# The opening of a two-layer kernel: whole first weight slab on ScalarE's queue, x tile 0 alone, and SyncE held by a dummy matmul

## The chip, the cores and the metric

One core of a Trainium2 chip runs the kernel. Its engines are TensorE (PE in the profile, its weight loads PEld), ScalarE (ACT), VectorE (DVE), GpSimd (POOL) and SyncE (SP); here SyncE only issues transfers. The metric is device time in microseconds (us), the median of several runs. Before the change it is 124.7 us (three runs, 124.55 to 125.05).

## The reference

```python
B, S, D, F = 1, 2048, 640, 1728          # all bfloat16
h = jnp.einsum("bsd,df->bsf", x, w1)     # x: (1, 2048, 640), w1: (640, 1728)
h = silu(h)
out = jnp.einsum("bsf,fd->bsd", h, w2)   # w2: (1728, 640)
```

## The kernel before

The contraction of the first product, D = 640, is cut into five k-tiles of 128. `xT` holds x turned, k on the partitions, and is filled by transposing transfers, which SyncE issues. `w1s` holds w1 with k on the partitions; a "slab" is the first 1024 columns of one k-tile (eight column tiles of 128, 256 KB). The 2048 rows are worked in four chunks of 512; an "x tile" below is one k-tile of the first chunk (512 rows by 128, 128 KB).

**The opening (first chunk).** Weights and x arrive in pieces, so the first chunk is worked k by k: for k = 0 to 4, TensorE goes over the eight column tiles and adds each product into that column's PSUM bank (`part`, `sweep`, `opening`). Each column tile is a pair of matmuls, one for each half of 64 columns (`step`). Step k waits for slab k and x tile k. After step 4 each bank goes through ScalarE's Silu into `hT`. Then come the remaining columns (`ld_rest`, `ld_rest2`), where one bank runs over all five k at once, then chunks 1 to 3 the same way, the last 64 columns, and the second product with its stores.

**Dummies.** Until the data is there TensorE multiplies a zeroed tile `z` (`first_dummies`): 13 full matmuls of 128 x 256 and one pair of half width.

**The order of the early work.** `early` takes what was just emitted and puts it ahead of the start barrier of its engine, so it runs at once. Each engine runs its own list in order. SyncE's list of early transfers is: x tiles 0 and 1 in one transposing transfer (L123); the last three eighths of slab 0 (L148); slabs 1 and 2 (L149, L150); x tile 2; slab 3; x tiles 3 and 4 in one; slab 4; then the rest of w1 in two pieces (L156, L157). After the barrier follow the transposing transfers of the other chunks (L163) and w2. ScalarE's early list is the first five eighths of slab 0 (L124) and a Silu on a small tile, which loads the activation table. All transfers of plain kind go through the helper `load` and so carry line 88; the early transposes carry line 93; all products carry line 175, the dummies line 132. A `wait` makes the engine's next instruction wait for a semaphore's value; each transfer has its own semaphore.

Of the kernel before, what the change touches and what calls it, by code (L numbers as in the profile page):

```python
# [9 lines left out]
def bass_standalone__dense_activation_silu__prompt_kernel(  # L10
# [13 lines left out]
    P = 128  # L24
    NB = 8
    BANK = 512
    DT = D // P
    FT = F // P
    FL = F - FT * P
    SCH = 512  # L30
    HB = 256
# [7 lines left out]
    pe, act, dve, pool, sp = nc.tensor, nc.scalar, nc.vector, nc.gpsimd, nc.sync  # L39

    with ExitStack() as es:
        def sb(name, shape, dtype):
            return es.enter_context(nc.sbuf_tensor(name, shape, dtype))
# [10 lines left out]
        z = sb("z", [P, HB], bf16)  # L54
        ps = es.enter_context(nc.psum_tensor("ps", [P, NB, BANK], fp32))
# [4 lines left out]
        def sem(name):  # L60
            s = es.enter_context(nc.semaphore(name))
            count[s.name if hasattr(s, "name") else name] = 0
            return [s, 0]

        def tick(ins, s, n=1):
            ins.then_inc(s[0], n)
            s[1] += n
            return (s, s[1])

        def wait(eng, *points):  # L70
            for pt in points:
                if pt is None:
                    continue
                s, v = pt
                key = (id(eng), id(s))
                if seen.get(key, 0) < v:
                    eng.wait_ge(s[0], v)
                    seen[key] = v

        s_pe, s_act, s_dve = sem("s_pe"), sem("s_act"), sem("s_dve")  # L80
# [4 lines left out]
        def load(eng, out_ap, in_ap):  # L85
            s = sem(f"s_ld{n_dma[0]}")
            n_dma[0] += 1
            return tick(eng.dma_start(out=out_ap, in_=in_ap), s, 16)

        def turned(c0, c1, k0, k1):  # L90
            s = sem(f"s_tr{n_dma[0]}")
            n_dma[0] += 1
            return tick(sp.dma_start_transpose(
                out=xT[:, k0:k1, c0:c1], in_=xf[c0:c1, k0 * P:k1 * P]), s, 16)

        ET = mybir.EngineType

        def early(emit, engine, arrived=True):
            n = len(nc.main_func.blocks[0].instructions)
            r = emit()  # L100
            lst = nc.main_func.blocks[0].instructions
            new = lst[n:]
            del lst[n:]
            at = next(
                i for i, ins in enumerate(lst)
                if ins.opcode == ("EventSemaphore" if arrived else "Drain") and ins.engine == engine
            )
            lst[at:at] = new
            return r
# [2 lines left out]
        w2_v = w2[0:F0, :].rearrange("(ft p) d -> p ft d", p=P)  # L112

        NO = NB
        NA = 5
        CO = NO * P

        def slab(eng, k, f0=0, f1=NO):
            return load(eng, w1s[:, k, f0 * P:f1 * P], w1_v[:, k, f0 * P:f1 * P])

        ld_w1 = {}
        ld_t = {}
        ld_t[0] = ld_t[1] = early(lambda: turned(0, SCH, 0, 2), ET.SP, False)  # L123
        ld_w1[0] = early(lambda: slab(act, 0, 0, NA), ET.Activation, False)  # L124
        p_z = early(lambda: tick(dve.memset(z[:, :], 0.0), s_dve), ET.DVE, False)  # L125

        bank_free = [None] * NB
# [1 line left out]
        def dummies(n, w):  # L129
            for _ in range(n):  # L130
                for c0 in range(0, P, w):
                    pe.matmul(ps[c0:c0 + w, 3, 0:HB], lhsT=z[:, 0:w], rhs=z[:, :],  # L132
                              start=True, stop=True)

        def first_dummies():
            wait(pe, p_z)
            dummies(13, P)
            dummies(1, HC)

        p_warm = early(lambda: tick(pool.memset(warm[:, :], 0.0), s_pool), ET.Pool, False)  # L140
# [4 lines left out]

        early(warm_up, ET.Activation, False)

        ld_w1b = early(lambda: slab(sp, 0, NA, NO), ET.SP, False)  # L148
        ld_w1[1] = early(lambda: slab(sp, 1), ET.SP, False)  # L149
        ld_w1[2] = early(lambda: slab(sp, 2), ET.SP, False)  # L150
        ld_t[2] = early(lambda: turned(0, SCH, 2, 3), ET.SP, False)
        ld_w1[3] = early(lambda: slab(sp, 3), ET.SP, False)
        ld_t[3] = ld_t[4] = early(lambda: turned(0, SCH, 3, DT), ET.SP, False)
        ld_w1[4] = early(lambda: slab(sp, 4), ET.SP, False)
        CM = CO + 2 * P
        ld_rest = early(lambda: load(sp, w1s[:, :, CO:CM], w1_v[:, :, CO:CM]), ET.SP, False)  # L156
# [17 lines left out]
        def mm(o, l, r, start, stop, shared=False):  # L174
            return pe.matmul(o, lhsT=l, rhs=r, start=start, stop=stop, skip_group_check=shared)  # L175
# [7 lines left out]
        def step(b, k, ft, c0, c1, start=False, stop=False):  # L183
            for h0 in (0, HC):
                ins = mm(ps[h0:h0 + HC, b, :], w1s[:, k, ft * P + h0:ft * P + h0 + HC],
                         xT[:, k, c0:c1], start, stop, shared=True)
            return ins

        def part(k, ft, c0, c1, start=False, stop=False):
            return step(ft, k, ft, c0, c1, start, stop)  # L190

        def sweep(k, c0, c1, *waits):
            wait(pe, *waits)
            for ft in range(NO):
                part(k, ft, c0, c1)

        def opening():
            first_dummies()
            wait(pe, ld_t[0], ld_w1[0])
            for ft in range(NO):  # L200
                if ft == NA:
                    wait(pe, ld_w1b)
                part(0, ft, 0, SCH, start=True)
            for k in range(1, DT - 1):
                sweep(k, 0, SCH, ld_w1[k], ld_t[k])

        early(opening, ET.PE)
        wait(pe, ld_w1[4], ld_t[4])
        for ft in range(NO):
# [12 lines left out]
        for ft in range(NO, FT):  # L222
# [3 lines left out]
            for k in range(DT):  # L226
                ins = step(b, k, ft, 0, SCH, start=(k == 0), stop=(k == DT - 1))
            silu(hT[:, ft, 0:SCH], ps[:, b, :], b, tick(ins, s_pe))
        for c in range(1, NSC):
            wait(pe, ld_xc[c])  # L230
            for ft in range(FT):
                b = bank()
                for k in range(DT):
                    ins = step(b, k, ft, c * SCH, (c + 1) * SCH, start=(k == 0), stop=(k == DT - 1))
                h_last = silu(hT[:, ft, c * SCH:(c + 1) * SCH], ps[:, b, :], b, tick(ins, s_pe))
        h_tail = []
        for q in range(NSC // 2):
            b = bank()
            for k in range(DT):
                for hh in range(2):  # L240
                    c = 2 * q + hh
                    ins = mm(ps[hh * FL:(hh + 1) * FL, b, :], w1s[:, k, F0:F],
                             xT[:, k, c * SCH:(c + 1) * SCH],
                             start=(k == 0), stop=(k == DT - 1), shared=True)
# [130 lines left out]
        for u, eng in ((A, dve), (B, act), (C, act), (E, dve), (G2, act)):  # L375
            for ft in range(FT):
                ins = u.whole(ft, ft == FT - 1)
# [30 lines left out]
```

## Time and profile before

| | |
|---|---|
| median of three runs | 124.7 us |
| profiled execution: its span, first to last instruction (the page has no other time for it) | 123.8 us |
| TensorE matmul busy | 121.3 us, 98% |
| ScalarE busy | 38.8 us, 31% |
| VectorE busy | 6.9 us, 6% |
| transfers of SyncE's queue | 10.11 MB, 34.1% of 16 DMA engines' span |
| transfers of ScalarE's queue | 0.16 MB, 0.6% |
| granted clock of TensorE, mean | 1.000 |

The profile is of one execution. A row names line, engine, operation and tile (written <- read), a count, and durations. In the view in order of time, a row gives start and duration in us, and in brackets the idle time ahead of it and what ended it; consecutive instructions of one kind are merged. An SPq or ACTq row is the issuing of a transfer, not its movement; the list of transfers gives the time from the start of the issue to the landing. In the view of stretches, a row gives the stretch, its length, an engine's busy time with its number of instructions, the granted clock, the mean share of the DMA engines and the GB/s. Some matmul records can be missing from a trace.

### The profile page before, as it was taken

The page shows a single profiled execution, that of the slowest core. Times are in us where ns is not written, and L with a number is a line of the kernel's source. Part 1 is how long each engine was busy: PE and PEld are TensorE (multiplying, and loading weights), DVE is VectorE, ACT ScalarE, POOL GpSimd, SP SyncE. Part 2 cuts the span into 40 slices and gives each one's busy share as a digit, 9 for nine tenths or more (in the row PEclk, how much of TensorE's full clock was granted, in tenths as well). Part 3 has the DMA queues.
Part 4 walks back from the last instruction along what each step waited for, and adds up shares of the span by engine and source line. Part 5 has one row for each costly group of instructions (what it writes and reads, how often), then busy time and mean ns, then how long its engine had stood idle before and what let it go on. Part 6 is the DMA issues. An engine that isn't in the chain of part 4 may idle for free.

```text
span 123.8 us, 2298 instructions
## 1 busy us (share of the span) xinstructions
PE 121.3 (98%) x1056; PEld 58.9 (48%) x1057; DVE 6.9 (6%) x11; ACT 38.8 (31%) x67; POOL 0.3 (0%) x5
## 2 busy tenths in 40 slices
PE   8999999999999999999999999999999999999993
PEld 5345545545545545545544444444444444444452
DVE  0000000000000000000000022002200300222001
ACT  4000985555555555555530011001100200110110
POOL 0000000000000000000000000000000000000000
DMA  6999974554894000000000004302200220023112
GB/s 138 239 246 331 138 86 91 100 77 107 214 394 157 0 0 0 3 5 0 0 0 5 0 0 101 74 0 105 107 0 5 106 106 0 5 106 116 53 66 82
DMA packets 19625, 10.42 MB, mean 84 GB/s; under 512 B 13728, under 2 KB 19104, under 8 KB 19616
## 3 DMA queue, kind: packets, MB, share of 16 engines
q1 hardware_dynamic: 19472, 10.11, 34.1%
q10 hardware_dynamic: 144, 0.16, 0.6%
q8 instruction: 8, 0.13, 0.5%
q14 instruction: 1, 0.01, 0.0%
HBM read 4.51 MB, written 2.62 MB: 58 GB/s over the span
## 4 chain that ended last, share of the span: by engine, by line
PE 95%; DMA 3%; ACT 0%; issue 0%
PE ps L175 95%; DMA xT<-in_x_dram 3%; ACT o_sb L256 0%
## 5 line engine op out<-in xcount | busy, mean ns | idle before, releaser
L175 PE MATMUL ps<-xT,w1s 128*64 128x512 bf16 x540 | 59.6, 384 | 0.1
L175 PE MATMUL ps<-w2s,hT 64*128 64x512 bf16 (+3 forms) x376 | 46.0, 369 | 0.2 <-issue 0.2
L175 PEld LDWEIGHTS ps<-xT,w1s 128*64 128x64 bf16 x540 | 30.0, 111 | 29.6 <-issue 1.2
L179 ACT ACTIVATE hT<-ps 128x512 bf16<-128x512 f32 x52 | 30.0, 607 | 29.9 <-PE ps L175 29.9
L175 PEld LDWEIGHTS ps<-w2s,hT 64*128 64x128 bf16 (+1 forms) x377 | 21.0, 95 | 24.2 <-issue 0.2
L256 ACT CAST o_sb<-ps 128x512 bf16<-128x512 f32 (+1 forms) x9 | 5.0, 551 | 41.5 <-PE ps L175 41.5
L175 PE MATMUL ps<-hT,w2s 64*128 64x512 bf16 x104 | 11.7, 376 | 0.0
L175 PEld LDWEIGHTS ps<-hT,w2s 64*128 64x128 bf16 x104 | 5.0, 94 | 6.3 <-issue 0.4
L254 DVE CAST o_sb<-ps 128x512 bf16<-128x512 f32 (+1 forms) x8 | 5.4, 675 | 40.5 <-PE ps L175 40.5
L254 DVE CAST oT<-ps 128x512 bf16<-128x512 f32 x2 | 1.4, 692 | 74.2 <-PE ps L175 74.2
L256 ACT CAST oT<-ps 128x512 bf16<-128x512 f32 x2 | 1.2, 586 | 10.6 <-PE ps L175 10.6
L132 PE MATMUL ps<-z 128*128 128x256 bf16 (+1 forms) x15 | 3.3, 419 | 0.4 <-DVE z L125 0.4
L175 PE MATMUL ps<-w2t,hTt 64*128 64x512 bf16 (+2 forms) x17 | 2.9, 363 | 0.0
L132 PEld LDWEIGHTS ps<-z 128*128 128x128 bf16 (+1 forms) x15 | 1.9, 142 | 1.5 <-issue 0.4
L179 ACT ACTIVATE hTt<-ps 128x512 bf16<-128x512 f32 x2 | 1.2, 598 | 1.0 <-PE ps L175 1.0
L144 ACT ACT_TABLE_LOAD x1 | 1.3, 1283 | 0.5 <-issue 0.5
L175 PEld LDWEIGHTS ps<-w2t,hTt 64*128 64x128 bf16 x17 | 0.9, 94 | 1.1
L175 PE MATMUL ps<-hTt,w2t 64*128 64x512 bf16 x4 | 0.8, 376 | 0.0
L175 PEld LDWEIGHTS ps<-hTt,w2t 64*128 64x128 bf16 x4 | 0.2, 94 | 0.2
L144 ACT ACTIVATE warm<-warm 128x32 f32<-128x32 f32 x1 | 0.2, 229 | 0.0
L125 DVE MEMSET z<- 128x128 uint32 x1 | 0.2, 165 | 0.2 <-issue 0.2
L140 POOL MEMSET warm<- 128x32 f32 x1 | 0.1, 125 | 0.0
(4 smaller groups left out, 0.4 us busy)
## 6 DMA issues: line engine op xcount, KB each, us to landing
out_dram<-o_sb SPq DMA_DIRECT2D x15, 160.0 KB, 1.8
w2s<-in_w_dram SPq DMA_DIRECT2D x1, 1120.0 KB, 6.1
w1s<-in_w_dram SPq DMA_DIRECT2D x4, 256.0 KB, 4.1
w2s<-in_w_dram SPq DMA_DIRECT2D x1, 960.0 KB, 8.2
w1s<-in_w_dram SPq DMA_DIRECT2D x1, 560.0 KB, 7.0
w1s<-in_w_dram SPq DMA_DIRECT2D x1, 320.0 KB, 5.8
xT<-in_x_dram SPq DMA_TRANSPOSE x18, 3.7
w1s<-in_w_dram ACTq DMA_DIRECT2D x1, 160.0 KB, 2.7
```

The costliest lines, as they stand in the source:

```text
L125: p_z = early(lambda: tick(dve.memset(z[:, :], 0.0), s_dve), ET.DVE, False)
L132: pe.matmul(ps[c0:c0 + w, 3, 0:HB], lhsT=z[:, 0:w], rhs=z[:, :], start=True, stop=True)
L140: p_warm = early(lambda: tick(pool.memset(warm[:, :], 0.0), s_pool), ET.Pool, False)
L144: act.activation(out=warm[:, :], in_=warm[:, :], func=ACT.Silu)
L175: return pe.matmul(o, lhsT=l, rhs=r, start=start, stop=stop, skip_group_check=shared)
L179: r = tick(act.activation(out=out_ap, in_=in_ap, func=ACT.Silu), s_act)
L254: r = tick(dve.tensor_copy(out=out_ap, in_=in_ap), s_dve)
L256: r = tick(act.copy(out=out_ap, in_=in_ap), s_act)
```

## The change

- ScalarE loads all of slab 0 in one transfer; SyncE's transfer of its last three eighths goes, and so does the wait for it after the fifth column tile.
- x tiles 0 and 1 are two transfers. Tile 0 is SyncE's first. Ahead of tile 1 SyncE waits for a semaphore that TensorE raises at the end of the fifth dummy. Then follow, in this order, tile 1, slabs 1 and 2, tile 2, slab 3, tiles 3 and 4 in one transfer, slab 4, and the rest as before. The wait stands ahead of all of these in SyncE's list.
- The full dummies are 11, five and six, where there were 13; the pair of half width stays.

```diff
-        NA = 5
         CO = NO * P
@@
-        ld_t[0] = ld_t[1] = early(lambda: turned(0, SCH, 0, 2), ET.SP, False)
-        ld_w1[0] = early(lambda: slab(act, 0, 0, NA), ET.Activation, False)
+        p_gate = (s_pe, 1)
+        ld_t[0] = early(lambda: turned(0, SCH, 0, 1), ET.SP, False)
+        ld_w1[0] = early(lambda: slab(act, 0), ET.Activation, False)
         p_z = early(lambda: tick(dve.memset(z[:, :], 0.0), s_dve), ET.DVE, False)
@@
         def dummies(n, w):
             for _ in range(n):
                 for c0 in range(0, P, w):
-                    pe.matmul(ps[c0:c0 + w, 3, 0:HB], lhsT=z[:, 0:w], rhs=z[:, :],
-                              start=True, stop=True)
+                    ins = pe.matmul(ps[c0:c0 + w, 3, 0:HB], lhsT=z[:, 0:w], rhs=z[:, :],
+                                    start=True, stop=True)
+            return ins
 
         def first_dummies():
             wait(pe, p_z)
-            dummies(13, P)
+            assert tick(dummies(5, P), s_pe) == p_gate
+            dummies(6, P)
             dummies(1, HC)
@@
-        ld_w1b = early(lambda: slab(sp, 0, NA, NO), ET.SP, False)
+        early(lambda: wait(sp, p_gate), ET.SP, False)
+        ld_t[1] = early(lambda: turned(0, SCH, 1, 2), ET.SP, False)
         ld_w1[1] = early(lambda: slab(sp, 1), ET.SP, False)
         ld_w1[2] = early(lambda: slab(sp, 2), ET.SP, False)
         ld_t[2] = early(lambda: turned(0, SCH, 2, 3), ET.SP, False)
         ld_w1[3] = early(lambda: slab(sp, 3), ET.SP, False)
-        ld_t[3] = ld_t[4] = early(lambda: turned(0, SCH, 3, DT), ET.SP, False)
+        ld_t[3] = ld_t[4] = early(lambda: turned(0, SCH, 3, 5), ET.SP, False)
         ld_w1[4] = early(lambda: slab(sp, 4), ET.SP, False)
@@
             wait(pe, ld_t[0], ld_w1[0])
             for ft in range(NO):
-                if ft == NA:
-                    wait(pe, ld_w1b)
                 part(0, ft, 0, SCH, start=True)
```

## The prediction

> **What bounds the kernel now.** I read the chain of work that ended last first, then the waits of the opening, then the opening in order of time, then stretches of it. The page's own chain and the same chain in order of time:
>
> ```profile
> PE 95%; DMA 3%; ACT 0%; issue 0%
> ```
> ```profile
> 0.00 3.78 DMA xT<-in_x_dram
> 3.78 0.04 issue
> 3.82 106.78 PE ps L175 x706
> ```
> From 3.82 us on TensorE works without a gap for 106.78 us. So the end moves only with (a) the moment of the first product, (b) TensorE's speed, (c) a gap that the change opens. What it edits lies in the first 8 us. There, in order of time (start, duration):
>
> ```profile
> 0.00 1.33 SPq L93 DMA_TRANSPOSE xT<-in_x_dram  x1
> 0.12 0.37 ACTq L88 DMA_DIRECT2D w1s<-in_w_dram  x1
> ...
> 0.39 3.31 PE L132 MATMUL ps<-z 128*128 128x256 bf16 x15 [0.39 <-DVE z L125]
> ...
> 1.39 1.54 SPq L88 DMA_DIRECT2D w1s<-in_w_dram  x3
> ...
> 2.97 1.16 SPq L93 DMA_TRANSPOSE xT<-in_x_dram  x1
> ...
> 4.17 0.58 SPq L88 DMA_DIRECT2D w1s<-in_w_dram  x1
> ...
> 4.79 1.24 SPq L93 DMA_TRANSPOSE xT<-in_x_dram  x1
> ...
> 6.07 1.62 SPq L88 DMA_DIRECT2D w1s<-in_w_dram  x3
> ```
> The two x tiles of the first transfer land at 3.78, the dummies end at 3.70, ScalarE's part of slab 0 has landed at 0.12 + 2.7 = 2.9: the x tiles are last. The next view gives TensorE's pace, by stretches (busy us, instructions):
>
> ```profile
> 5.53:5.96 0.43, 0.43 (x6) 1.00 1.98 298
> 5.96:6.30 0.34, 0.34 (x4) 1.00 0.77 115
> 6.30:6.52 0.22, 0.22 (x6) 1.00 0.81 231
> ```
> Each stretch is the pitch of one pair of products: 0.427 us up to 5.96, 0.216 from 6.30, one pair between at 0.34. The column of the granted clock says 1.00 throughout and doesn't show this. With c us at the slow pace in the mixed pair, c/0.427 + (0.34 - c)/0.216 = 1 gives c = 0.26: TensorE doubles its pace at 6.22. From 3.82 to there 5.6 of slab 0's eight pairs run slow; the step over slab 0 ends at 6.74, the later steps take 1.73 each and begin at 6.74, 8.46, 10.19 and 11.92, and the columns after the eighth begin at 13.64.
>
> **What it is measured against.** The profiled span is 123.8; the median of the runs is 124.7 (124.55 to 125.05), 0.9 more, for what lies around the span. I add the change of the span to 124.7. Half a per cent, 0.62 us, is about what a measurement of this kernel can tell from no change.
>
> **Part 1: tile 0 alone, slab 0 whole on ScalarE, two dummies fewer.** The first product waits for tile 0 and all of slab 0. The dummies took 2.89 us from 0.39 to the half pair at 3.28, 0.22 each; two fewer put that pair at 2.84, so 3.06 is the earliest start. The latest: before, 160 + 256 KB had to land for it, now 256 + 128 KB. The queues moved 241 GB/s from 1.78 to 3.30; 32 KB less is 0.14, so data at 3.64 and a start at 3.68 (the 0.04 of issue included). I take a value between. The missing tile is worth 128 KB / 241 = 0.54. ScalarE's extra 96 KB goes partly into room that stood free: in the quarters from 1.25 the rates were 128, 230 and 220 GB/s, where 286 came right after, room for (158 + 56 + 66) x 0.25 = 70 KB. Some 26 KB, 0.11, are left: 3.78 - 0.54 + 0.11 = 3.35, and I start the products there. Slab 0 with that load comes at 2.9 + 96 KB / 241 = 3.27, also before.
>
> The Trainium skill, "DMA: Bandwidth & Descriptors", Rules for kernel authors, speaks against this part: transfers issued from several engines run on the same 16 DMA engines, so spreading them saves issue time alone. By that rule, taken strictly, the start is the byte-bound 3.68. The trace doesn't decide: 416 KB arriving by 3.78 fits it, the low rate before 1.75 leaves room.
>
> Starting 0.47 earlier isn't 0.47 of the end, because those microseconds run at the slow pace. With the doubling still at 6.22: (6.22 - 3.35)/0.427 = 6.7 pairs slow, 1.3 x 0.216 = 0.28 after, the step ends at 6.50 and not 6.74: **0.24 less**. Ends: start 3.06 gives 0.38, start 3.68 gives 0.07.
>
> "TensorE: Matmul & The Clock Gate" of the Trainium skill, Part 1, says that the gate opens after a window of some 3.4 us of activity and that the windows run freely, whatever the kernel does; by it the doubling stays where it is when work is moved inside the window, so 0.24 and not 0.47. It also says the phase differs from run to run. The three runs of before lie within 0.5 us, which bears out no wide spread.
>
> **Part 2: SyncE's order.** Slab 0's last 96 KB (one issue, some 0.6 with its gap) leave the queue; tile 1 becomes an issue of its own (1.16, as the one-tile transfer at 2.97 has it), held until the fifth dummy is done: 0.39 + 4 x 0.22 + 0.42 = 1.69. SyncE would be free at 1.2 to 1.3, so 0.4 of the hold is real. Behind it everything is queued: tile 1 at 1.69 to 2.85, slab 1 at 2.91 (was 2.00), slab 2 at 3.44 (2.49), tile 2 at 3.97, slab 3 at 5.17, tiles 3 and 4 at 5.79, slab 4 at 7.07, the two rests about 7.7 and 8.2, the five transposes of the next chunk from 9.1 (8.09). So all is issued about 1.0 later. This part costs nothing as long as the landings keep ahead of TensorE; the cover is the lead that each had.
>
> From issue to landing before: slab 1 3.9, slab 2 4.1, tile 2 4.2, slab 3 4.1, tiles 3 and 4 4.4, slab 4 4.5, the rests 5.8 and 7.0. Upper end, those latencies unchanged: slab 1 lands at 6.81 against a need at 6.50, 0.31 late; tile 2 8.17 against 8.23; tiles 3 and 4 10.2 against 9.95, 0.25 late, but hidden if slab 1 was already waited for; slab 4 11.6 against 11.68; the first rest 13.5 against 13.40, the second 15.2 against 15.6. The delays don't add, the largest counts: 0.35 with the wake-up. Lower end, none: ScalarE's transfer at 0.12, with little ahead of it, needed 2.7 for 160 KB; 96 KB more are 0.41, so slab 1 could land at 2.91 + 3.1 = 6.0; tiles 3 and 4 with the first transfer's 3.8 at 9.6. I take none, nearer to the lower end: what kept slab 1 for 3.9 was two tiles and 96 KB ahead of it, now one tile that is gone by then. Tiles 3 and 4 at 9.6 to 10.2 against 9.95 are the thinnest lead. Tile 1 itself, at 1.69 + 3.8 = 5.5, is 1.0 ahead of its need at 6.50.
>
> **Part 3: small things at nothing.** The semaphore on the fifth dummy and the dropped wait inside slab 0 (its weights had landed at 5.3, its sixth pair went at 5.53 without a gap in the products) cost nothing either way. SyncE reaches the barrier at some 8.8, not 7.75; ScalarE's first real work is at 12.34 and TensorE needs its release before the step at 11.92, three us later. The next chunk's x landed by 17.0 and is needed at 13.64 + 5 x 1.08 = 19.04; its transposes begin 1.0 later, inside that cover of 2 us.
>
> **Sum:** 124.7 - 0.24 + 0 = **124.46**.
>
> **The rivals.**
> - **SyncE's hold is paid.** Slab 1 (or tiles 3 and 4) lands as late as its issue says. For it: latencies of 3.9 to 4.5 in every row. Against: they were measured in a fuller queue. Up to 0.35 of wait against 0.24 of gain: up to 124.8, about 124.65 in the middle. It turns to a loss once slab 1 lands after 6.74.
> - **The change doesn't bring the data earlier.** Bytes decide, start at 3.68: 124.7 - 0.07 = 124.63.
> - **The clock starts over: slower.** Place: the gap between the last dummy, now at 3.26 (3.70 - 0.44), and the first product. Before, it was 0.12 and TensorE kept its count: slow from 0.39 to 6.22, 5.83 long. If a longer gap, that is a start after about 3.4, makes it count anew from the first product at, say, 3.6, the slow pace lasts until 9.4, 3.2 us more at half speed: 1.6 lost, less the 0.1 gained: 126.2. Against: 0.12 did no harm, and the gap grows only if slab 0 is late.
> - **The clock comes with the products.** If the doubling follows the first product by the 2.40 seen, the whole 0.47 is won: 124.2; with a start at 3.06, 0.76: 123.9. For it: nothing but that the trace can't exclude it.
>
> **How the numbers follow.** Forecast 0.50 (own range 124.3 to 124.65), hold paid 0.22, data no earlier 0.08, clock anew 0.10, clock with the products 0.10. Nearly all of the first three is within half a per cent; I keep 0.08 of them for a loss past it (a later transfer behind the hold, which the latencies of before don't show) and 0.07 for a gain, since three runs spread 0.5. Half of the last case, 0.05, passes 0.62 as well. Slower 0.10 + 0.08 = 0.18, faster 0.07 + 0.05 = 0.12, within 0.70. The range, 124.0 to 125.3, holds all but the clock anew and the last case's far end; its upper end is the paid hold (124.8) and 0.5 for what else the delayed queue may hold up.
>
> **What would show it.** First product at 3.1 to 3.7, most likely 3.35, and 0.43 pitch until about 6.2; SyncE's tile 1 issued near 1.7 and its later issues 1.0 later; no gap of TensorE before the second step (near 6.5) and the fourth (near 9.95); the chain's first piece shorter by 0.47. Wrong if the pace doubles elsewhere than 6.2, or if weight loads wait for w1 or xT between 6 and 14 us by more than 0.24.

## The result and the profile after

The changed kernel takes 126.55 us in the median (124.84 to 126.70), the kernel before 124.56 (124.29 to 125.05), six runs each. The ratio on record is 1.0125, 95% interval 1.0092 to 1.0159; the two medians alone would give 1.016. The forecast was 124.46. The six times are two groups: 126.53, 126.56, 126.58 and 126.70, and 124.84 and 124.99, 1.7 apart. (Here and below medians and ranges hold all runs, while a ratio leaves out runs more than 1.5% above the fastest of their kernel: four of a_nogate's, five of b_act13's and two of b_split's.)

The profiled execution of the changed kernel is one of the first group (126.53, span 125.2). Its chain in order of time, and the opening in order of time (start, duration; the row at 1.67 is from a window of its own, in the long one it is merged with the first transfer):

```profile
0.00 4.01 DMA xT<-in_x_dram
4.01 0.04 issue
4.06 119.31 PE ps L178 x1041
```
```profile
0.39 2.88 PE L132 MATMUL ps<-z 128*128 128x256 bf16 x13 [0.39 <-DVE z L125]
...
1.67 1.15 SPq L93 DMA_TRANSPOSE xT<-in_x_dram  x1
...
2.86 1.05 SPq L88 DMA_DIRECT2D w1s<-in_w_dram  x2
3.96 1.13 SPq L93 DMA_TRANSPOSE xT<-in_x_dram  x1
4.06 14.16 PE L178 MATMUL ps<-xT,w1s 128*64 128x512 bf16 x108 [0.79 <-DMA xT<-in_x_dram]
```
The first product starts at 4.06, later than before (3.82), and still waits for x: tile 0 by itself landed at 4.01, where two tiles together had landed at 3.78. The dummies end at 3.27, so TensorE idles for 0.79 us. (Products are on line 178 now.) The pace of the pairs, as stretches with the busy time of TensorE:

```profile
7.90:8.32 0.42, 0.42 (x4) 1.00 1.08 254
8.32:8.75 0.43, 0.43 (x4) 1.00 1.28 271
8.75:8.98 0.23, 0.23 (x4) 1.00 1.34 340
8.98:9.20 0.22, 0.22 (x5) 1.00 1.09 277
```
By the same reckoning as in the prediction the pace doubles at 8.78, not at 6.22. That is the whole difference between the two profiled executions: the products run slow for 4.72 us instead of 2.40, and 2.32 x (1 - 0.216/0.427) = 1.15; with the 0.24 of the later start 1.39. The spans differ by 125.2 - 123.8 = 1.4. TensorE has no further wait in the first 20 us.

One correction to the scale. The runs now come with time and span, 126.53 beside 125.2 and 124.55 beside 123.2: 1.3 lies around a span, not 0.9. The profiled execution of before (123.8) was thus one of some 125.1, at the upper end of its runs. That is why the medians differ by 2.0 and the two spans by 1.4 only.

### The profile page after: what moved, and what is told of

It reads as the page before. It is cut to its first block, busy times and chain, and to the rows that moved or that the text cites. A ratio compares the mean times of both kernels' runs of the same rounds, so it can differ in the third digit from the quotient of the medians.

```text
span 125.2 us, 2296 instructions
## 1 busy us (share of the span) xinstructions
PE 122.2 (98%) x1055; PEld 59.9 (48%) x1055; DVE 6.9 (6%) x11; ACT 38.8 (31%) x67; POOL 0.3 (0%) x5
## 4 chain that ended last, share of the span: by engine, by line
PE 95%; DMA 3%; ACT 0%; issue 0%
PE ps L178 95%; DMA xT<-in_x_dram 3%; ACT o_sb L257 0%
## 5 line engine op out<-in xcount | busy, mean ns | idle before, releaser
L178 PE MATMUL ps<-xT,w1s 128*64 128x512 bf16 x540 | 60.8, 389 | 0.8 <-DMA xT<-in_x_dram 0.8
L178 PEld LDWEIGHTS ps<-xT,w1s 128*64 128x64 bf16 x540 | 31.3, 113 | 30.1 <-issue 2.7
```

## The experiments

Medians of the kernel before in the same batches were 124.44 to 124.63. The runs are grouped by question, not in the order in which they were run; each theory is spelled out in the expectations. In the diffs `@@` stands for lines left out; where a hold is new, `dummies` also returns its last matmul, as in the changed kernel.

**Is it the gap?** Four more dummies in the changed kernel:

```diff
-            dummies(6, P)
+            dummies(10, P)
```


> The changed kernel with four dummies more (5 + 10 + the half pair), so that they end near 4.1, where its first product started, and leave no gap. Theory G (the gap of 0.79 us between the last dummy and the first product costs TensorE its full pace for longer): the pace doubles before 7 us again instead of at 8.8 and all runs lie at 124.4 to 125.2. Rival P (the pace doubles a fixed time after the first product, 4.7 us in the changed kernel's profile): still 8.8, and 126.5. Rival N (what slows it is a difference between executions that has nothing to do with the gap): both times of the changed kernel, near 124.9 and near 126.6, are seen again.

Measured: 125.15 (124.57 to 125.43, ten runs), 1.0039 times the kernel before (1.0013 to 1.0066). The group near 126.6 is gone although the first product is only 0.06 earlier, so rival N falls. Half of the runs lie above the 125.2 that G allowed. Its opening:

```profile
0.39 3.31 PE L132 MATMUL ps<-z 128*128 128x256 bf16 x17 [0.39 <-DVE z L125]
4.00 1.92 PE L178 MATMUL ps<-xT,w1s 128*64 128x512 bf16 x16 [0.29 <-DMA xT<-in_x_dram]
6.11 1.92 PE L178 MATMUL ps<-xT,w1s 128*64 128x512 bf16 x16 [0.20 <-DMA w1s<-in_w_dram]
8.24 1.05 PE L178 MATMUL ps<-xT,w1s 128*64 128x512 bf16 x8 [0.21 <-DMA xT<-in_x_dram]
```
```profile
2.71:2.93 0.22, 0.22 (x3) 1.00 0.65 141
2.93:3.09 0.16, 0.16 (x2) 1.00 0.63 139
3.09:3.20 0.11, 0.11 (x3) 1.00 0.72 163
```
The second fence has stretches of one dummy's pitch each: in this execution the pace doubled at 3.04, among the dummies, a microsecond before any product. Rival P falls. And it shows what I had costed at nothing: with the fast pace from the start TensorE is at the second step (6.11) before slab 1 and at the third (8.24) before tile 2; from pair to pair each wait is 0.36 to 0.38 longer than the pitch.

**The gap without the change's transfers.** The kernel before with two, then four dummies fewer:

```diff
-            dummies(13, P)
+            dummies(11, P)     # b_gap; 9 in b_gap9
```


> The kernel before with two dummies fewer (11 and the half pair), nothing else: its transfers and so its first product (3.82) stay, and the gap ahead of it grows from 0.12 to 0.55 us. Theory G: if 0.55 is enough, some or all runs rise by about 1.7 to 126.2; if it isn't, 124.6 as before, and the bound lies between 0.55 and 0.79. Rivals P and N: 124.6, no change.

Measured: 124.80 (124.18 to 125.33, ten runs), ratio 0.9997 (0.9967 to 1.0026). In the profile the x tiles came at 3.57, so the gap was 0.35 and not the 0.55 expected, and the pace doubled at 4.32. A gap of this size costs nothing that shows in the ratio. But this execution, with its pace doubled 1.9 us earlier than in the first profile, was the slowest of the ten (125.33). The end of its chain says why the early doubling won nothing:

```profile
14.69 4.45 DMA xT<-in_x_dram
19.14 0.04 issue
19.18 102.97 PE ps L175 x911
```
TensorE reaches the second chunk before its x, the last of the five transposes of line 163, which lands at 19.14, and loses 0.89 us there from pair to pair. That transfer then sets the end, and not the opening.

> The kernel before with four dummies fewer (9 and the half pair), transfers untouched: the dummies end at 2.85, the first product stays at 3.6 to 3.8, so the gap is 0.8 to 1.0 us, as in the changed kernel. Theory G (a gap of 0.7 us or more costs the pace, 0.55 doesn't): most of the runs rise to 126 or more, others stay near 124.5, the median is above 125.5, and a profile of a slow run shows the pace doubling after 7.3. If the changed kernel's loss came from its transfers, 124.6.

Measured: 125.94 (125.17 to 126.92, eight runs), ratio 1.0119 (1.0076 to 1.0162). Four dummies alone, with every transfer as before, cost as much as the whole change. The first lines of its opening, and the stretch where its pace doubles, at 7.08:

```profile
0.39 2.45 PE L132 MATMUL ps<-z 128*128 128x256 bf16 x11 [0.39 <-DVE z L125]
3.71 5.50 PE L175 MATMUL ps<-xT,w1s 128*64 128x512 bf16 x34 [0.86 <-DMA xT<-in_x_dram]
```
```profile
6.70:7.10 0.40, 0.40 (x4) 1.00 1.04 261
7.10:7.32 0.22, 0.22 (x4) 1.00 1.00 289
```

**The hold.** First without it, then with the semaphore on the ninth dummy:

```diff
-        early(lambda: wait(sp, p_gate), ET.SP, False)      # a_nogate
```
```diff
-            assert tick(dummies(5, P), s_pe) == p_gate     # a_gate9
-            dummies(6, P)
+            assert tick(dummies(9, P), s_pe) == p_gate
+            dummies(2, P)
```


> The changed kernel without the wait on the fifth dummy: tile 1 is issued at 1.3 instead of 1.67 and all behind it 0.4 earlier. Theory T (tile 0 lands late, 4.01, because tile 1's packets are already in the queue when its last writes finish): tile 0 lands no earlier than 3.9, the gap of TensorE stays at 0.7 or more, and the time stays near 126.5. Rival L (tile 0 is late because ScalarE's 256 KB go ahead of it, and tile 1 does nothing): tile 0 at 4.0 as well, so this run alone doesn't tell the two apart; it says whether the hold does anything at all.

Measured: 125.97 (124.37 to 126.91, ten runs), ratio 1.0044 (0.9999 to 1.0089). Tile 0 at 3.95, first product at 4.00, gap 0.72, pace doubled at 7.95. Tile 0 is where both T and L expected it, the median is 0.5 under T's 126.5; the hold at 1.67 changes next to nothing for tile 0 (4.01 with it).

> The changed kernel with the hold on the ninth dummy instead of the fifth: tile 1 is issued at 2.5 instead of 1.67, all behind it 0.85 later. Theory T: tile 0 lands at 3.1 to 3.4, the first product starts there, the gap behind the dummies shrinks to 0.1, the pace doubles before 7 us, but tile 1 (landing near 5.3) and slab 1 (issued at 3.7, landing 6.7 to 7.1) may hold the second step for up to 0.5: 124.3 to 125.0. Rival L: tile 0 still lands near 4.0, and 126.5 or more.

Measured: 126.17 (125.77 to 127.33, four runs), ratio 1.0130 (1.0059 to 1.0201). Tile 0 came at 3.60, 0.4 earlier than with tile 1 close behind it, but not at the 3.1 to 3.4 that T alone wanted. The gap was 0.37 and the pace doubled at 5.65; the time is as bad as the changed kernel's, for another reason:

```profile
3.65 2.88 PE L178 MATMUL ps<-xT,w1s 128*64 128x512 bf16 x16 [0.37 <-DMA xT<-in_x_dram]
6.92 2.45 PE L178 MATMUL ps<-xT,w1s 128*64 128x512 bf16 x20 [0.39 <-DMA w1s<-in_w_dram]
```
SyncE's queue is 0.85 later again, slab 1 lands at 6.87, and TensorE loses 0.55 us waiting for it, from pair to pair; then 0.64 more at 19.96, where the second chunk's x comes last, as in b_gap. The expectation of 124.3 to 125.0 was wrong in that.

**What makes tile 0 late.** All of slab 0 on ScalarE in the kernel before; and the reverse, 160 KB in the changed one:

```diff
-        ld_w1[0] = early(lambda: slab(act, 0, 0, NA), ET.Activation, False)      # b_whole
+        ld_w1[0] = early(lambda: slab(act, 0), ET.Activation, False)
@@
-            dummies(13, P)
+            dummies(15, P)
@@
-        ld_w1b = early(lambda: slab(sp, 0, NA, NO), ET.SP, False)
@@
-                if ft == NA:
-                    wait(pe, ld_w1b)
```
```diff
-        ld_w1[0] = early(lambda: slab(act, 0), ET.Activation, False)             # a_160, beside the hold on the ninth dummy
+        ld_w1[0] = early(lambda: slab(act, 0, 0, 5), ET.Activation, False)
@@
         ld_t[1] = early(lambda: turned(0, SCH, 1, 2), ET.SP, False)
+        ld_w1b = early(lambda: slab(sp, 0, 5, NO), ET.SP, False)
@@
+                if ft == 5:
+                    wait(pe, ld_w1b)
```


> The kernel before with all of slab 0 on ScalarE (the last three eighths leave SyncE), tiles 0 and 1 still in one transfer and no hold; 15 dummies in place of 13, so that a later first product leaves no long gap. Theory L (ScalarE's larger slab is what makes the x tiles land late): tiles 0 and 1 land at 4.0 to 4.2 instead of 3.6 to 3.8, the first product 0.3 later, but slab 1 and all behind it are issued 0.6 earlier, and the time is 124.3 to 124.8. Rival T (only tile 1's packets delay tile 0): the tiles land at 3.6 to 3.8 as before, 124.2 to 124.5.

Measured: 125.05 (124.29 to 125.45, ten runs), ratio 1.0028 (1.0000 to 1.0057). The two tiles land at 4.16, where ScalarE's 160 KB had let them land at 3.78 (before), 3.57 (b_gap) and 3.67 (b_gap9). The landing is L's; the time misses L's 124.3 to 124.8.

> The changed kernel with the hold on the ninth dummy, and only five eighths of slab 0 on ScalarE; the last three eighths go on SyncE behind tile 1, so the sixth column tile of the first step waits for them. This asks only when tile 0 lands with 160 KB beside it and nothing behind it; its time says little (the sixth column waits till 6 or so). Theory L: 3.0 to 3.3, where 256 KB gave 3.60. If the size of ScalarE's slab does nothing: 3.5 to 3.6 again.

Measured: tile 0 at 3.10, where 256 KB gave 3.60; L. (Its time, 127.24 in two runs, is set by the sixth column tile, which waited 1.3 us.) The list of transfers has the same issue in this kernel, in the one with 256 KB, and in the changed kernel (last column: us to landing), one fence each:

```profile
xT<-in_x_dram SPq DMA_TRANSPOSE x1, 3.1
```
```profile
xT<-in_x_dram SPq DMA_TRANSPOSE x1, 3.6
```
```profile
xT<-in_x_dram SPq DMA_TRANSPOSE x1, 4.0
```
So of the 0.9 between 3.1 and 4.0 the larger slab makes 0.5 and tile 1 close behind it 0.4. Each figure is from one profile; with tile 1 close behind, tile 0 landed at 4.01 and 3.98 (the changed kernel twice), 3.95 (a_fill), 3.95 (a_nogate) and 3.83 (a_nogate_fill).

**Without the hold and without the gap.** The two edits together:

```diff
-            dummies(6, P)
+            dummies(10, P)
@@
-        early(lambda: wait(sp, p_gate), ET.SP, False)
```


> The changed kernel without the hold and with 15 dummies and the half pair. With the hold and the same dummies the median was 125.15, 0.6 over the kernel before, and its profile shows TensorE waiting for slab 1 and tile 2 for about 0.35 each time. Theory S (that rest is SyncE's later queue): the queue runs 0.4 earlier, so the waits shrink to 0.1 or less and the time falls to 124.6 to 124.9. Rival: the rest comes from the first product being 0.2 later, and the time stays at 125.0 to 125.3.

Measured: 124.73 (124.35 to 125.77, ten runs), ratio 1.0038 (1.0005 to 1.0072); the median falls by 0.4 from a_fill's, the ratio doesn't. The profile, of the slowest of the ten, does not bear S out where S looked: the wait for slab 1 at 6.08 is 0.41 from pair to pair, against 0.36 in a_fill, and slab 1 lands at 6.04 against 6.07 although it was issued 0.28 earlier. Its largest wait is another, 1.00 for the second chunk's x at 19.63. S stays open.

**More on ScalarE.** If SyncE's queue is what limits an execution with an early doubling, slabs 1 and 3 could go on ScalarE's (b_act13, shown), and tile 0 alone with it (b_split: these edits and those of the last experiment below):

```diff
-        ld_w1[1] = early(lambda: slab(sp, 1), ET.SP, False)
+        ld_w1[1] = early(lambda: slab(act, 1), ET.Activation, False)
@@
-        ld_w1[3] = early(lambda: slab(sp, 3), ET.SP, False)
+        ld_w1[3] = early(lambda: slab(act, 3), ET.Activation, False)
```


> The kernel before with slabs 1 and 3 issued by ScalarE behind its warm-up activation (from 2.05) instead of by SyncE; the first product and the dummies stay. SyncE's later issues come 0.5 earlier from slab 2 on and 1.1 earlier from tiles 3 and 4 on. Theory S (in executions in which the pace doubles early TensorE outruns the transfers, and SyncE's queue sets the time there): the fast end falls, 123.9 to 124.3, the median to 124.2 to 124.4. If the transfers are bound by the DMA engines and not by the issuing, 124.5 as before or worse.

Measured: 126.03 (124.77 to 128.62, twelve runs), ratio 1.0068 (1.0036 to 1.0100).

> The run before it, and tile 0 alone: SyncE issues tile 0, the last three eighths of slab 0, tile 1, slab 2, tile 2 and so on; ScalarE has five eighths of slab 0 and, behind its warm-up, slabs 1 and 3; 11 dummies and the half pair; no hold. With 160 KB beside it tile 0 landed at 3.10 in an earlier run. Theory L: first product at 3.1 to 3.3, no gap; where the pace doubles late this wins up to 0.3, where it doubles early slab 1 and tile 1 (near 5) set the second step: median 124.0 to 124.4. Rival T (what follows tile 0 in the queue delays it too): tile 0 at 3.5 to 3.8, the gap at 0.3 to 0.5, 124.4 to 125 with single slow runs.

Measured: 126.50 (124.71 to 126.98, eleven runs), ratio 1.0109 (1.0071 to 1.0148). Both fail at one place, seen in the first's opening:

```profile
0.55 1.28 ACT L144 ACT_TABLE_LOAD   x1 [0.55 <-issue]
0.61 0.87 ACTq L88 DMA_DIRECT2D w1s<-in_w_dram  x2
1.85 0.23 ACT L144 ACTIVATE warm<-warm 128x32 f32<-128x32 f32 x1
4.59 6.67 PE L175 MATMUL ps<-xT,w1s 128*64 128x512 bf16 x60 [0.89 <-DMA xT<-in_x_dram]
```
The slabs stand behind the warm-up activation in ScalarE's list, but are issued at 0.61, while the activation runs at 1.85: it follows the load of its table, which ends at 1.83, and the issues don't. So what was said ahead of the prediction, that each engine runs its own list in order, does not hold for these issues: they go out ahead of the activation. With them in flight the x tiles land at 4.54 (b_split: tile 0 at 4.10, where the last experiment, without the two slabs on ScalarE, has it at 3.16; gap 0.87, doubling at 8.70).

> The kernel before with slabs 1 and 3 on ScalarE, but held there until the seventh dummy is done (2.1): in the run without this hold they were issued at 0.61, not behind the warm-up activation as I had thought, and pushed the x tiles from 3.7 to 4.54. Theory S+L: tiles 0 and 1 land at 3.6 to 3.9 again, the gap stays under 0.4, no run over 125.5; SyncE's issues from tile 2 on are 0.5 to 1.1 earlier, so no wait for the weights or x in the second to fourth step, and the median falls to 124.2 to 124.4, under both kernels. Rival: the slabs of the two queues interleave and slab 1 lands later than the 5.88 of before; 124.5 to 124.9.

This is b_act13 with ScalarE waiting for the seventh dummy's semaphore ahead of slab 1:

```diff
-            dummies(13, P)
+            assert tick(dummies(7, P), s_pe) == (s_pe, 1)
+            dummies(6, P)
@@
+        early(lambda: wait(act, (s_pe, 1)), ET.Activation, False)
         ld_w1[1] = early(lambda: slab(act, 1), ET.Activation, False)
```
Measured: 125.42 (124.76 to 125.57, nine runs), ratio 1.0052 (1.0024 to 1.0081). The x tiles are back at 3.76 and no run passes 125.57. But the rival is right in its mechanism, and the median is above its 124.9: with two queues at work slab 0's last part comes at 6.30 instead of 5.24 and slab 1 at 6.80 instead of 5.88, and TensorE waits 1.27 us inside the first step.

```profile
3.80 1.27 PE L178 MATMUL ps<-xT,w1s 128*64 128x512 bf16 x10
...
6.34 14.00 PE L178 MATMUL ps<-xT,w1s 128*64 128x512 bf16 x128 [1.27 <-DMA w1s<-in_w_dram]
```

**The changed kernel again.**

> The changed kernel as it is, for more executions and a second profile. Theory F (the pace is decided over stretches of about 3.4 us whose place differs from execution to execution, and a stretch in which TensorE idles for more than some 0.85 us doesn't double it): two groups again, most runs at 126 to 127, some at 124.4 to 125.3; first product at 3.9 to 4.1; in the profile the pace doubles either before 4.1 or after 7.3, never between 4.2 and 7.2. A doubling inside 4.2 to 7.2 with a gap over 0.7 would refute it.

Measured: 126.72 (126.02 to 126.93, four runs). First product at 4.03, gap 0.76, and the pace doubles at 9.62, where the first profile of the same kernel had 8.78 with the product at 4.06. So the moment differs between executions; as F says, it lies after 7.3. The lower group that F expected beside it was not seen in these four runs.

**Tile 0 alone, nothing else.**

```diff
-        ld_t[0] = ld_t[1] = early(lambda: turned(0, SCH, 0, 2), ET.SP, False)
+        ld_t[0] = early(lambda: turned(0, SCH, 0, 1), ET.SP, False)
@@
-            dummies(13, P)
+            dummies(11, P)
@@
         ld_w1b = early(lambda: slab(sp, 0, NA, NO), ET.SP, False)
+        ld_t[1] = early(lambda: turned(0, SCH, 1, 2), ET.SP, False)
```


> The kernel before with tile 0 alone and 11 dummies, nothing else of the change: ScalarE keeps its five eighths of slab 0, SyncE issues tile 0, the last three eighths, tile 1, slab 1, slab 2, tile 2 and so on, without a hold, each about 1.2 later than before. Theory L (the larger slab on ScalarE's queue made tile 0 late): first product at 3.1 to 3.3, gap under 0.2, no group of runs near 126.6; executions in which the pace doubles early wait for slab 1 or tile 1, so 124.3 to 125.0 in the median. Rival T (whatever follows tile 0 in the queue delays it): first product at 3.6 or later.

Measured: 125.32 (124.87 to 126.37, twelve runs), ratio 1.0068 (1.0043 to 1.0092).

```profile
0.39 2.88 PE L132 MATMUL ps<-z 128*128 128x256 bf16 x13 [0.39 <-DVE z L125]
3.21 6.12 PE L176 MATMUL ps<-xT,w1s 128*64 128x512 bf16 x40
```
L, clearly: tile 0 lands at 3.16 and there is no gap. Here tile 1 stood behind a plain transfer. And yet it is 0.7 slower: a first product 0.6 earlier wins nothing. In this profile (span 123.9) the pace doubled at 6.52, 0.30 later than in the first profile, and slab 4 lands at 11.89, for which TensorE loses 0.18; what the later queue costs in the executions that double early was not profiled for this kernel. Single runs reach 126.4, which I did not expect and cannot explain.

No variant beat the kernel before.

## Why the prediction was wrong

**What failed first: the start of the first product,** taken at 3.35 between ends of 3.06 and 3.68; measured 4.06 and 4.03. Two terms of it were mis-sized. ScalarE's extra 96 KB were put at 0.11, since 70 KB of them were to go into free room; 160 against 256 KB under the same hold measured 0.50. And tile 1 was put at nothing for tile 0: its 128 KB were taken off whole, 0.54. But the hold ends at 1.67, when tile 0 had over a microsecond to go, and tile 1 close behind cost 0.4 (hold on the ninth dummy: 3.60). My upper end was no end either, for the same reason: counting bytes at one rate gave 3.64 for the data without tile 1, and 3.60 was measured when tile 1 was kept away; with its 128 KB counted in, the same reckoning gives 4.19, an estimate, and 4.01 was measured. The Trainium skill's rule of "DMA: Bandwidth & Descriptors", Rules for kernel authors, that transfers of several queues share the 16 DMA engines, points the right way; b_whole, b_act13 and a_160 bear it out, with 0.4 to 1.0 us on the x tiles.

**What turned 0.24 of delay into 1.4 us: the doubling.** This was a rival, "the clock starts over", at a chance of 0.10 and 126.2; the group at 126.5 to 126.7 is its place, and near its size. Three of its details were wrong. Its point was put too low: a gap above 0.12, a start after 3.4. The gap grew because tile 0 was late, not slab 0, which had landed at 2.92. And TensorE does not count 5.83 us anew from the first product: behind the long gaps the doubling came 3.37 to 5.59 us after it, and in b_act13 ahead of it; that the rival's size came out near is in part luck. Measured doublings, by the gap of the same profile:

| kernel | gap, us | pace doubles at |
|---|---|---|
| b_tile0 | none | 6.52 |
| before, b_whole | 0.12, 0.08 | 6.22, 6.34 |
| a_fill | 0.29 | 3.04 |
| b_gap, a_gate9 | 0.35, 0.37 | 4.32, 5.65 |
| a_nogate | 0.72 | 7.95 |
| after, again | 0.79, 0.76 | 8.78, 9.62 |
| b_gap9, b_split | 0.86, 0.87 | 7.08, 8.70 |
| b_act13 | 0.89 | inside the gap, by 4.6 |
| a_nogate_fill, b_act13_held | none, 0.14 | ahead of the first product, by 3.9 and 3.8 |
| a_160 | none, but 1.32 inside the first step, up to 6.81 | 9.69 |

Up to 0.37 the pace doubles by 6.52 at the latest; from 0.72 it doubles by the end of the gap or not before 7.08. b_gap9 against b_gap, with the same transfers, shows that the gap does it; the number of dummies does not, since b_gap and the changed kernel have the same. "TensorE: Matmul & The Clock Gate" of the Trainium skill, Part 1, describes freely running windows of 3.4 us, of which a busy one opens the gate. The table fits that: the changed kernel's two groups are 1.7 us apart, which is what a window of 3.4 us at half pace costs, as an estimate. The windows themselves are in no view here, and where between 0.37 and 0.72 the bound lies was not tried.

**What I had read out of three runs.** That they lie within 0.5 us I took as evidence against a moment that differs between executions. It differs: 3.04 to 6.52 without a long gap. The spread of the times stays small, as far as the profiles show, because an early doubling runs into data that hasn't landed: slab 1 and tile 2 in a_fill, the second chunk's x in b_gap and a_nogate_fill.

**SyncE's queue** was issued as forecast to within 0.06: tile 1 at 1.67 (1.69), slab 1 at 2.86 (2.91), slab 3 at 5.14 (5.17), tiles 3 and 4 at 5.75 (5.79), slab 4 at 7.05 (7.07), the next chunk's at 9.09 (9.1). Slab 1 landed at 6.28, inside 6.0 to 6.81, tiles 3 and 4 at 9.64, inside 9.6 to 10.2; slab 4 at 11.96 was past its upper end of 11.6. It cost nothing in the profiled execution, because TensorE was slow and late. Where it isn't, the rival "SyncE's hold is paid" holds too: a_fill stands 0.4% over the kernel before, with waits for slab 1 and tile 2 in its profile. **The small things** at nothing were right in that execution: no wait inside slab 0, none at the barrier, none for the next chunk. But the cover of the next chunk was misread: in the first profile its last transpose, issued at 14.57, lands 3.4 later, at 18.0 and not at 17.0, so the lead was 1.0 and not 2, as much as the change takes. Wherever the pace doubled early this lead could be used up, as b_gap, a_gate9 and a_nogate_fill show.

## What to carry to other kernels

Work that only keeps TensorE busy until the data comes must be cut to when the data does land, not to when it is hoped to: here dummies that ended 0.35 us early cost nothing that shows (b_gap), 0.76 to 0.87 us early over 1% (the changed kernel, b_gap9, b_split). A transfer put on a second queue to free the first was paid for here by what was in flight on the first at that moment; measure the landing of the one transfer that the start waits for. And before a bound on an earlier start is turned into a gain, ask what TensorE meets next: here it met slabs that had been put later, and the second chunk's x.

## What was not expected of the hardware

The moment at which TensorE's pace doubles ranged from 3.04 to 9.69 us over these profiles while the column of the granted clock said 1.00 in all of them. Only one of the traces, a_gate9's, holds a record of that clock at all: full rate from 5.63 on, beside the 5.65 read off the pitch; so 1.00 ahead of that is no reading. A ScalarE issue that stands behind an activation goes out 1.2 us ahead of it (0.61 against 1.85). The same single x tile, issued at 0.00, landed at 3.10 to 4.10 by what else was in flight.
